# An attention and feed-forward block on one core: the last denominators by stream shuffles, the score bounds as 128 x 128, and a new tile table

## The chip, the cores and the metric

The kernel runs on one core of one Trainium2 chip. The time is the device time of the core in microseconds, the median of several runs. The profile comes from one execution, whose own time is given beside its span.

## The reference

```python
xn = layernorm(x)                       # x: 1 x 2048 x 512, bf16
q = (xn @ wq) -> 32 heads of 16;  k = xn @ wk;  v = xn @ wv   # one k and v of width 16 for all heads
p = softmax(q k^T / 4)                  # 32 x 2048 x 2048
A = (p v, heads joined) @ wo
B = gelu(xn @ w1 + b1) @ w2 + b2        # hidden width 1792
out = x + A + B
```

## The kernel before, in words

**Tiles.** Scores are made transposed: a tile has 128 keys on its rows and 512 columns of queries of one head. There are 2048 such tiles, in 32 groups of 64 tiles; a group has four heads (`j`, one in each 32-row block of PE's array) and sixteen key blocks. A unit `u` is three tiles that follow each other, three banks of PSUM; two sets of three banks alternate, so the scores (`scores`, L986) of a unit wait until the tiles two units earlier have been read.

**Two ways to the exponential.** The string `DTAB` says for each unit which of its tiles go to VectorE (DVE) rather than ScalarE (ACT). ACT takes its tiles of a unit in one instruction (`exp`, L1009). For a DVE tile, `p1` (L1040) turns the score into an integer whose bits are a rough exponential in bf16, and frees the bank. Up to six such tiles form a batch (`close_batch`), and additions (L1087 on DVE, two for a batch; L1083 one for each tile, on GpSimd (POOL) or DVE) make three shifted copies; five products with scaled values stand for one tile. A character of `DTAB` out of `CLOSE` ends a batch early. The products with V (`pv_mm`, L1053) add up in one bank, `pO`: each head has sixteen rows of output and one row, 16 of its 32, with the denominator.

**Score bounds.** Row 16 of each head's block in `QT` holds a bound that is subtracted from the scores. `q_pack` projects the queries of eight heads into bank 7 (`pM`), copies them out (`qp`, L1190), squares them (`sqq`, L1191) and spreads `qp` to `QT` by DMAs. `q_m` sums the squares with a selector `sel8R`, one matmul of 512 columns into 32 rows for each `p`, in the first of four column groups; DVE turns the sums into bounds (`mT`, L1203, 32 x 512), and four DMAs on SyncE's (SP's) queue put the rows into `QT`. `q_m` is called nine times, with 16 matmuls in all.

**Denominators.** For all groups but the last, `pO` is copied out (`o_evac` L1134, `o_quarter` L1100), the denominators go through DRAM to be inverted and spread, and a product follows (L1162, L1122; on POOL, or DVE where the planner puts it). The last group has `o_norm_last`: DVE copies `pO` in two halves (L1169), PE spreads the denominator row with a selector `selB` (f32, L675), ACT takes the logarithm (L1176) and the exponential of its negative (L1179), and DVE multiplies (L1182). Then sixteen matmuls with `wol`, a copy on ACT (L1407) and the last store follow.

**Order.** All work is recorded as operations with dependencies. `Prog.schedule` plays them through with assumed durations and picks by due time; the order found is the order of each engine's instructions, and `emit` adds the semaphores. The feed-forward work is spread over the units by the tables `HP` and `YP` (unit numbers). PE's idle gaps can be given filler matmuls (L1414). A planner constant, `C_OCC`, is what a 512-column matmul of one column group is taken to last.

Of the kernel before, what the change touches and what calls it, by code (L numbers as in the profile page):

```python
# [10 lines left out]
P = 128  # L11
# [13 lines left out]
C_OCC = 0.197  # L25
C_FIRST = 0.0105
WIN = 3.413
HAM_T = 0.35
# [34 lines left out]
CLOSE = "otABX"  # L63
DTAB = "tot00t2.0to2.o.0t20.o22ot02..t22t000ot..2o.o202.ot.02.o02oo2o.0oo0.00t.222t.2t2.o202.222t2o..2t0.ttt220o2.t.22.0o0o0.o2t.t02o0o.2t0t000.tt00.o2o0.2t0t.02oo22o.02o.22o2.o0o0..222o2ttttxxxB2t20.o20o0.o2t22oo2.t20o.ott0002.t0.t20.ot20oo02.t0200022t220.oo22.oo.t..o202t.t2o20to00..t022o0o0.20.t002.t0.0.022t.o2.0t.2t0t22t0.o0t.220o02t22.00o..2.22ot2.t0.2t0ot0t.02.oo0t22o20.0tt2220t.t02..0t222o.o0o.2t0o0ttt..20oo022t2.o0ot2..0oto.0t2t220o0t02.2oo20.2.o.22oo2o.o02.0o2t2t0.t.222o.o.2t2220ot..202o.02o0t0t2t.222tt022abXXAo02t22o0.o0..0o0o22t.t200tt2..t2t00ot.2o20ooo2o2.o20.o202.o.0t2to00ot2.t00ot0o.0.t.0tt020.t.oto2o02t2220.22o20t.2o0o202o.22..t22t00to202.0ooo2..0.0to.t2tt0o0ot0.t..0.."
YF = 664
# [12 lines left out]
QK = ((48,88.7,157.4),(45,107.7,130.4),(62,118.7,159.4))  # L78
HP = ((37,14,56.70835,151,34.34256,79.56046,20.54375,16.61271,55,117.24185,34.04239,145.57386,53.56559,74.35212),(146.29246,86.86647,89.5731,104.42399,169,0,0,0,0,0,0,0,0,0),(265,317.59193,277.51784,331,247,313,283,279.40403,337.07508,415,309.45685,269.66744,457,498.66805),(477.33471,482.59711,471.81669,494.32464,434.68696,0,0,0,0,0,0,0,0,0))
YP = ((199,183,217.4734,241),(346.51102,360.57108,380.86188,410.65667),(539.99266,523.90597,567.16436,582.95092),(593.39845,625,654.09462,657.83105))  # L80
GU = tuple((u, tbs, n, (("s", tbs[0], 0, 7), ("p", tbs[1], 5, 3), ("s", tbs[0], 7, 7), ("p", tbs[1], 8, 1), ("p", tbs[1], 9, 1),
# [24 lines left out]
TBW = 512  # L106
# [11 lines left out]
class Prog:  # L118
# [114 lines left out]
    def schedule(self):  # L233
# [43 lines left out]
        while left:  # L277
# [113 lines left out]
            if e == "pe":  # L391
                vleft -= op.kind == "v"
                s_seen = s_seen or vleft == 0
                st = t
                if op.kind in ("pv", "side"):
                    cg = op.tag[1]
                    st = max(t, cgbusy[cg], free["pe"])
                    if mode != "col":
                        st = r1 = max([t, pend + SW_COL] + [c + SW_COL for c in cgbusy])
                    op.start = st  # L400
                    cgbusy[cg] = st + (C_OCC + (C_FIRST if st < r1 + 0.1 else 0.0)) * slow
                    area += 0.0533
                    recent.append((st, 0.0533))
                    op.end = st + 0.006
                    op.vis = st + op.occ * slow + op.lat
                    mode = "col"
                    g = op.tag[0]
                if op.kind == "pv":
                    n = accn[g] = accn[g] - 1
                    s = started.setdefault(g, {})  # L410
                    s[cg] = s.get(cg, 0) + 1
                    op.tag = (g, cg, s[cg] == 1)
                    if len(s) == 4:
                        opened = g
                    if n == 0:
                        opened = None
                elif op.kind != "side":
                    m = {"S": "row", "side": "col"}.get(op.kind, "full")
                    w = 0.0 if m == mode else SW_ROW if m == "row" else SW_COL if m == "col" else SWITCH
                    st = max([t, pend + w] + [c + w for c in cgbusy])  # L420
                    op.start = st
                    op.end = st + op.occ * slow
                    op.vis = op.end + op.lat
                    area += op.occ * (0.75 if op.kind == "S" else 1.0)
                    recent.append((st, op.occ * (0.75 if op.kind == "S" else 1.0)))
                    if m == "col":
                        cgbusy = [op.end] * 4
                    mode = m
            else:
                op.start = t  # L430
                op.end = t + op.occ
                op.vis = op.end + op.lat
            if e == "pe":
                while op.start > wend:
# [3 lines left out]
                    area, wend = 0.0, wend + WIN  # L438
                pend = op.start + (C_OCC if op.kind in ("pv", "side") else op.occ) * slow
            if e == "act" and op.kind in ("exp", "gelu"):  # L440
# [30 lines left out]
    def settle(self):  # L471
        free = {e: 0.0 for e, _ in self.SECTIONS}
        mode, cg, pend, aend, r1 = None, [0.0] * 4, 0.0, 0.0, 0.0
        for op in self.ops:
# [3 lines left out]
            if op.eng == "pe":  # L478
                if op.kind in ("pv", "side") or (op.kind == "fill" and occ > 0.15):
                    if mode != "col":  # L480
                        t = r1 = max([t, pend + SW_COL] + [c + SW_COL for c in cg])
                    else:
                        t = max(t, cg[op.tag[1]])
                    cg[op.tag[1]] = t + C_OCC + (C_FIRST if t < r1 + 0.1 else 0.0)
                    mode, end = "col", t + 0.006
                else:
# [3 lines left out]
                    mode, end = m, t + occ  # L490
                pend = t + (C_OCC if mode == "col" else occ)
            else:
# [53 lines left out]
def bass_parallel_sum__grouped_kv_mqa__dense_activation_gelu__prompt_kernel(  # L546
# [33 lines left out]
    with ExitStack() as es:  # L580
# [28 lines left out]
        ident_f = sb([P, P], f32, "ident_f")  # L609
        selB = sb([P, P], f32, "selB")  # L610
        isc = sb([P, 1], f32, "isc")
# [38 lines left out]
        def bank(b, n=1):  # L650
            return pAll[:, b * 512:(b + n) * 512]
# [49 lines left out]
        def setup(fn, r=(), w=(), occ=0.16, due=0.0, lat=0.1, **kw):  # L701
# [23 lines left out]
        setup(lambda e: e.tensor_copy(ident_f[:], ident[:]), r=["ident"], w=["ident_f"], due=9.0)  # L725
        sel_diag = [bass.AP(sel8[:].tensor, sel8[:].offset + gl, [list(sel8[:].ap[0]), [34, NGR // 2], [8, HG]])
                    for gl in range(2)]
# [14 lines left out]
        for gl in range(2):  # L742
            setup(lambda e, gl=gl: e.tensor_copy(sel_diag[gl], mask8[:, 4 * gl:4 * gl + 4].unsqueeze(1).to_broadcast([P, NGR // 2, HG])),
                  r=["mask8", "sel8"], w=["sel8"], due=12.0)
# [178 lines left out]
        for v in KV_ORD:  # L923
# [5 lines left out]
            else:  # L929
# [4 lines left out]
        late = [pr.writer["ibi"]]  # L934
        setup(lambda e: e.tensor_copy(selB[:].rearrange("p (j r) -> p j r", j=4), ident[:, 16:113:32].unsqueeze(2).to_broadcast([P, 4, 32])),
              r=["ident"], w=["selB"], occ=0.3, due=24.0, after=late)
        dma("sp", wop[:], A_wo.rearrange("(g p) n -> p g n", p=P), "d_wo", w=["wop"], after=late)
# [228 lines left out]
        def o_norm_last(gg):  # L1166
            for h in range(2):
                c = slice(h * 256, h * 256 + 256)
                dve(lambda e, c=c: e.tensor_copy(Of[:, 1, c], pO[:, c]), w=["O", ("Of", 1), ("Of", 2 + h)], n=256, due=0.0)  # L1169
            for h in range(2):  # L1170
                c = slice(h * 256, h * 256 + 256)
                mm(bank(h)[:, 0:256], selB[:], Of[:, 1, c], True, True, r=[("Of", 2 + h), "selB"], w=[B(h)], occ=0.44, due=0.0)
            RB = [("rbP", 0, h, j) for h in range(2) for j in range(HG)]
            for h in range(2):
                c = slice(h * 256, h * 256 + 256)
                act(lambda e, h=h, c=c: e.activation(rbP[:, 0, c], bank(h)[:, 0:256], ACT.Ln), w=[B(h), ("rbl", h)] + RB, n=256, due=0.0)  # L1176
            for h in range(2):
                c = slice(h * 256, h * 256 + 256)
                act(lambda e, c=c: e.activation(rbP[:, 0, c], rbP[:, 0, c], ACT.Exp, scale=-1.0), w=[("rbl", h)], n=256, due=0.0)  # L1179
            for h in range(2):  # L1180
                c = slice(h * 256, h * 256 + 256)
                dve(lambda e, c=c: e.tensor_tensor(oT[:, c], Of[:, 1, c], rbP[:, 0, c], ALU.mult),  # L1182
                    r=[("Of", 2 + h), ("rbl", h)], w=[("oTl", h)], n=256, due=0.0)

# [14 lines left out]
        def q_m(ps, hqs):  # L1199
            for n, p in enumerate(ps):  # L1200
                mm(pM[0:32, :], sel8R[:, p, :], sqq[:, p % 2, :], n == 0, n == len(ps) - 1, r=["sel8R", ("sq", p % 2)],
                   w=[M4[0]], tp=(0, 0), kind="side", tag=(None, 0))
            dve(lambda e: e.tensor_scalar(mT[:].bitcast(i16), pM[0:32, :].bitcast(i32),  # L1203
                                          0.5 / 65536.0, float(0x1fc00000) / 65536.0, ALU.mult, ALU.add),
                w=M4 + ["mT"], allow=EV_ALLOW)
            h0, n = hqs[0], len(hqs)
            for j in range(HG):
                dma("sp", QT[32 * j + 16:32 * j + 17, h0:h0 + n, :], mT[8 * j + h0:8 * j + h0 + n, :], "d_m",
                    r=["mT"], w=[("QTm", hq, j) for hq in hqs])

# [242 lines left out]
```

## Time and profile before

| what | value |
|---|---|
| median of 3 runs | 744.11 us (744.03 to 744.12) |
| profiled execution | 743.81 us |
| its span | 742.1 us, 22084 instructions |
| PE busy | 729.0 us, 9117 matmuls |
| DVE busy | 727.0 us, 1374 instructions |
| ACT busy | 728.4 us, 759 instructions |
| POOL busy | 407.1 us, 554 instructions |
| granted TensorE clock | 1.000 |

Busy time counts what one or more instructions of an engine cover. Instructions overlap the ones behind them a little, so an engine can be held up by less than the overlap without showing idle time. In a row of groups stand the source line, engine, operation, output and inputs, shape and count, then busy microseconds and the mean nanoseconds of one, then the idle time ahead of them. In a row of the timeline stand start and length in microseconds.

### The profile page before, as it was taken

How to read it: one execution, taken by the hardware profiler on the slowest of the kernel's cores; microseconds unless marked ns; L12 is line 12 of the kernel's file. 1: busy time of each engine (PE TensorE's matmuls, PEld its weight loads, DVE VectorE, ACT ScalarE, POOL GpSimd, SP SyncE). 2: the span in 40 equal slices, each digit the busy share in tenths (PEclk: the TensorE clock that was granted, in tenths of full speed). 3: DMA queues.
4: the chain of work that ended last, by engine and by line, in shares of the span. 5: the costliest groups of instructions: out<-in, count | busy, mean ns of one | idle time of the engine just before them, and what ended most of it. 6: DMA issues, size and time to landing. Idle time of an engine off the chain costs nothing.

```text
span 742.1 us, 22084 instructions
## 1 busy us (share of the span) xinstructions
PE 729.0 (98%) x9117; PEld 229.8 (31%) x9117; DVE 727.0 (98%) x1374; ACT 728.4 (98%) x759; POOL 407.1 (55%) x554
## 2 busy tenths in 40 slices
PE   7999999999999999999999999999999999999998
PEld 4333322322243323222232323232233323223232
DVE  8899999999999999999999999999999999999995
ACT  8999999999999999999999999999999999999996
POOL 5565565666526565465566346564643575564642
PEclk9999999999999999999999999999999999999999
DMA  9200100100011020101101010010101101100010
GB/s 313 63 16 16 31 11 17 25 9 19 9 30 32 9 53 17 31 11 34 35 7 34 24 39 23 11 31 9 25 10 28 28 23 39 31 24 25 15 38 24
DMA packets 35963, 23.54 MB, mean 32 GB/s; under 512 B 17361, under 2 KB 32281, under 8 KB 35865
## 3 DMA queue, kind: packets, MB, share of 16 engines
q1 hardware_dynamic: 34808, 22.12, 11.6%
q8 instruction: 72, 1.18, 0.7%
q14 instruction: 27, 0.21, 0.1%
q10 hardware_dynamic: 1056, 0.03, 0.1%
HBM read 13.28 MB, written 2.35 MB: 21 GB/s over the span
## 4 chain that ended last, share of the span: by engine, by line
ACT 58%; PE 36%; DVE 5%; DMA 0%; issue 0%; SPq 0%
ACT E L1009 58%; PE pAll L1053 17%; PE pAll L986 11%; PE pAll L681 7%; DVE Dt L1040 1%; DVE Dt L1087 1%; DVE stats L770 1%; PE pAll L675 1%; DMA x_sb<-in_A_x_dram 0%; PE pAll L1414 0%; DVE ub L806 0%; ACT xnT L826 0%; DVE Dt L1083 0%; ACT ub L803 0%; DVE mv L784 0%
## 5 line engine op out<-in xcount | busy, mean ns | idle before, releaser
L1009 ACT ACTIVATE E<-pAll 128x1024 bf16<-128x1024 f32 (+1 forms) x678 | 675.6, 1187 | 2.7 <-PE pAll L986 2.5
L1083 POOL TENSOR_SCALAR Dt<-Dt 128x512 int16<-128x512 int16 x470 | 367.2, 781 | 301.5 <-DVE Dt L1087 130.3
L1053 PE MATMUL pAll<-Dt,V 128*32 128x512 bf16 x2845 | 430.5, 383 | 1.0 <-DVE Of L1134 0.8
L1040 DVE TENSOR_SCALAR Dt<-pAll 128x512 int16<-128x512 f32 x555 | 376.5, 694 | 2.3 <-PE pAll L986 1.1
L1087 DVE TENSOR_SCALAR Dt<-Dt 128x1024 int16<-128x1024 int16 (+8 forms) x514 | 292.4, 592 | 0.2
L1053 PE MATMUL pAll<-E,V 128*32 128x512 bf16 x1479 | 282.9, 385 | 0.0
L986 PE MATMUL pAll<-QT,KT 32*128 32x512 bf16 x2048 | 267.1, 384 | 2.8 <-ACT E L1009 1.6
L1053 PEld LDWEIGHTS pAll<-Dt,V 128*32 128x32 bf16 x2845 | 115.1, 94 | 120.9 <-issue 78.4
L986 PEld LDWEIGHTS pAll<-QT,KT 32*128 32x128 bf16 x2048 | 66.4, 90 | 275.6 <-ACT E L1009 257.7
L681 PE MATMUL pAll<-xnT,w_sb 128*32 128x512 bf16 x896 | 117.8, 382 | 0.0
L1053 PEld LDWEIGHTS pAll<-E,V 128*32 128x32 bf16 x1479 | 66.2, 94 | 44.0 <-issue 31.0
L681 PE MATMUL pAll<-w_sb,x_sb 128*32 128x512 bf16 x448 | 73.6, 381 | 0.0
L681 PE MATMUL pAll<-w_sb,ub 128*32 128x512 bf16 x448 | 72.6, 382 | 0.0
L681 PEld LDWEIGHTS pAll<-xnT,w_sb 128*32 128x32 bf16 x896 | 33.5, 95 | 21.8 <-issue 9.8
L681 PE MATMUL pAll<-wop,oTp 128*32 128x512 bf16 x192 | 34.7, 384 | 0.0
L1083 DVE TENSOR_SCALAR Dt<-Dt 128x512 int16<-128x512 int16 x99 | 25.5, 282 | 0.0
L1162 POOL TENSOR_TENSOR oTp<-OfP,rbP 128x256 bf16<-128x256 f32 x23 | 18.5, 814 | 7.6 <-DVE Dt L1087 4.4
L681 PE MATMUL pAll<-xnT,wq_sb 128*32 128x512 bf16 x256 | 21.1, 383 | 0.5 <-DVE ub L1218 0.5
L681 PEld LDWEIGHTS pAll<-w_sb,x_sb 128*32 128x32 bf16 x448 | 19.8, 95 | 4.0 <-issue 1.4
L1218 DVE TENSOR_SCALAR ub<-pAll,b1T 128x512 bf16<-128x512 f32 x28 | 20.8, 741 | 0.1
L681 PEld LDWEIGHTS pAll<-w_sb,ub 128*32 128x32 bf16 x448 | 19.2, 95 | 4.1 <-issue 2.3
L681 PE MATMUL pAll<-b2row,ones 128*32 128x512 bf16 x60 | 17.6, 383 | 0.0
(125 smaller groups left out, 273.9 us busy)
## 6 DMA issues: line engine op xcount, KB each, us to landing
w_sb<-in_B_w_dram SPq DMA_DIRECT2D x2, 1792.0 KB, 13.1
OfP<-Of SPq DMA_DIRECT2D x96, 32.0 KB, 1.9
rbP<-rden_rows SPq DMA_DIRECT2D x96, 32.0 KB, 1.8
x_sb<-in_A_x_dram SPq DMA_DIRECT2D x8, 256.0 KB, 4.3
x_sb<-in_A_x_dram SPq DMA_DIRECT2D x16, 128.0 KB, 2.3
QT<-qp SPq DMA_DIRECT2D x124, 16.0 KB, 1.8
out_dram<-x_sb SPq DMA_DIRECT2D x15, 128.0 KB, 1.9
OfP<-Of SPq DMA_DIRECT2D x56, 16.0 KB, 1.8
```

Source lines behind the costliest of these rows:

```text
L675: return add("pe", lambda e: e.matmul(o, l, rh, start=start, stop=stop, **kw), r, w, occ=occ, lat=dlat[1], allow=allow, **ak)
L681: add("pe", lambda e, c=c, j=j: e.matmul(o[c, :], l[:, c], rh, start=start, stop=stop, tile_position=(0, 32 * j)), r, [(k, j) for k in w] ...
L770: dve(lambda e, ti=ti, c=c: e.bn_stats(stats[:, c, :], x_sb[:, ti, :]), r=[("x", ti)], w=[("st", ti)], n=511, due=land(ti) + DU["sd"])
L986: ins = e.matmul(o, l, rh, start=True, stop=True, tile_position=(q0, 0))
L1009: o = act(lambda e: e.activation(E[:, s0:s0 + na, :], bank(b0, na).rearrange("p (a n) -> p a n", a=na), ACT.Exp, scale=LN2 / 128.0), w=[B( ...
L1040: op = dve(lambda e: e.tensor_scalar(Dt[:, s:s + n, :], bank(bk, n).rearrange("p (a n) -> p a n", a=n), float(127 * 128) + SPL_D, SPL_MIN, ...
L1053: add("pe", lambda e, a, b: e.matmul(pO[32 * j:32 * j + 32, :], V1[:, v, kt, :], rhs, start=a, stop=b, tile_position=(0, 32 * j)), r=r + [ ...
L1083: add("pool", lambda e, d=d, k=k: e.tensor_scalar(d, d, 1.0, float(k), ALU.mult, ALU.add), [], [(("D", base[o > 0] + q), o)], occ=PL_OCC, ...
L1087: dve(lambda e, d=view(o, nb), q=view(i, nb), k=k: e.tensor_scalar(d, q, float(k), None, ALU.add), r=keys(i), w=keys(o), n=nb * n * TBW, m ...
L1162: "pool", lambda e, c=c: e.tensor_tensor(oTp[0:n, sl, c], OfP[0:n, s, c], rbP[0:n, s, c], ALU.mult),
L1218: dve(lambda e: e.tensor_scalar(ubs[tb % 2][:, ft, :], pM, b1T[:, ft:ft + 1], None, ALU.add), r=["b1T"], w=M4 + [ukey(tb, ft)], n=TBW + 57 ...
```

## The change

Three things change.

1. `o_norm_last`: DVE no longer copies `pO`; two stream shuffles read it and write row 16 of every 32-row block to all 32 rows of `Of`. ACT's logarithm and exponential work on `Of` in place, and the products read `pO` itself. The matmuls with `selB`, and `selB`, go.
2. `q_m`: for each `p`, four matmuls of 128 columns, one in each column group, take the place of one of 512. The bounds stand as 128 rows x 128 columns (four query blocks by 32 groups and heads), one eviction of that shape; `sel_diag` orders the selector's columns to suit. Four DMAs, one for each query block, write four rows of `QT` at once; where only some groups are wanted, there are four for each.
3. The tables `DTAB`, `HP` and `YP` are replaced, and the planner is given 0.06 for a short matmul (`M_OCC`).

```diff
+M_OCC = 0.06
-DTAB = "tot00t2.0to2.o.0t20..."
+DTAB = "oto00t0t..2otttt.0o..."
...
-HP, YP = ...
+HP, YP = ...
...
-                    cgbusy[cg] = st + (C_OCC + (C_FIRST if st < r1 + 0.1 else 0.0)) * slow
+                    cgbusy[cg] = st + (min(op.occ, C_OCC) + (C_FIRST if st < r1 + 0.1 else 0.0)) * slow
...
-    sel_diag = [... [[34, NGR // 2], [8, HG]] ...]
+    sel_diag = [... [[80, 2], [34, 2], [4, HG]] ...]
-        mT = sb([32, TBW], bf, "mT")
+        mT = sb([P, P], bf, "mT")
...
         def o_norm_last(gg):
-            for h in range(2):
-                dve(tensor_copy(Of[:, 1, c], pO[:, c]))
-            for h in range(2):
-                mm(bank(h)[:, 0:256], selB[:], Of[:, 1, c])
-            for h in range(2):
-                act(activation(rbP[:, 0, c], bank(h)[:, 0:256], Ln))
-            for h in range(2):
-                act(activation(rbP[:, 0, c], rbP[:, 0, c], Exp, scale=-1.0))
-            for h in range(2):
-                dve(tensor_tensor(oT[:, c], Of[:, 1, c], rbP[:, 0, c], mult))
+            for h, c in enumerate(cs):
+                dve(stream_shuffle(Of[:, 1, c], pO[:, c], [16] * 32), n=300)
+            for h, c in enumerate(cs):
+                act(activation(Of[:, 1, c], Of[:, 1, c], Ln))
+            for h, c in enumerate(cs):
+                act(activation(Of[:, 1, c], Of[:, 1, c], Exp, scale=-1.0))
+            for h, c in enumerate(cs):
+                dve(tensor_tensor(oT[:, c], pO[:, c], Of[:, 1, c], mult))
...
         def q_m(ps, hqs):
             for n, p in enumerate(ps):
-                mm(pM[0:32, :], sel8R[:, p, :], sqq[:, p % 2, :], ..., tp=(0, 0))
-            dve(tensor_scalar(mT, pM[0:32, :], ...))
-            for j in range(HG):
-                dma("sp", QT[32 * j + 16:32 * j + 17, h0:h0 + n, :], mT[8 * j + h0:8 * j + h0 + n, :])
+                for c in range(4):
+                    mm(pM[32 * c:32 * c + 32, 0:P], sel8R[:, p, :], sqq[:, p % 2, P * c:P * c + P], ..., tp=(0, 32 * c), occ=M_OCC)
+            dve(tensor_scalar(mT, pM[:, 0:P], ...), n=P)
+            for c in range(4):
+                # n == 4: one DMA; otherwise one for each group of hqs
+                dma("sp", QT[16:113:32, h0:h0 + n, P * c:P * c + P], mT[32 * c + 4 * h0:32 * c + 4 * h0 + 16, :])
```

More of the change, by code (lines that the diff above doesn't have):

```diff
@@ L438, in schedule @@
                     area, wend = 0.0, wend + WIN
-                pend = op.start + (C_OCC if op.kind in ("pv", "side") else op.occ) * slow
+                pend = op.start + (min(op.occ, C_OCC) if op.kind in ("pv", "side") else op.occ) * slow
             if e == "act" and op.kind in ("exp", "gelu"):
@@ L483, in settle @@
                         t = max(t, cg[op.tag[1]])
-                    cg[op.tag[1]] = t + C_OCC + (C_FIRST if t < r1 + 0.1 else 0.0)
+                    cg[op.tag[1]] = t + min(occ, C_OCC) + (C_FIRST if t < r1 + 0.1 else 0.0)
                     mode, end = "col", t + 0.006
@@ L490, in settle @@
                     mode, end = m, t + occ
-                pend = t + (C_OCC if mode == "col" else occ)
+                pend = t + (min(occ, C_OCC) if mode == "col" else occ)
             else:
@@ L609, in bass_parallel_sum__grouped_kv_mqa__dense_activation_gelu__prompt_kernel @@
         ident_f = sb([P, P], f32, "ident_f")
-        selB = sb([P, P], f32, "selB")
         isc = sb([P, 1], f32, "isc")
@@ L725, in bass_parallel_sum__grouped_kv_mqa__dense_activation_gelu__prompt_kernel @@
         setup(lambda e: e.tensor_copy(ident_f[:], ident[:]), r=["ident"], w=["ident_f"], due=9.0)
-        sel_diag = [bass.AP(sel8[:].tensor, sel8[:].offset + gl, [list(sel8[:].ap[0]), [34, NGR // 2], [8, HG]])
+        sel_diag = [bass.AP(sel8[:].tensor, sel8[:].offset + gl, [list(sel8[:].ap[0]), [80, 2], [34, 2], [4, HG]])
                     for gl in range(2)]
@@ L934, in bass_parallel_sum__grouped_kv_mqa__dense_activation_gelu__prompt_kernel @@
         late = [pr.writer["ibi"]]
-        setup(lambda e: e.tensor_copy(selB[:].rearrange("p (j r) -> p j r", j=4), ident[:, 16:113:32].unsqueeze(2).to_broadcast([P, 4, 32])),
-              r=["ident"], w=["selB"], occ=0.3, due=24.0, after=late)
         dma("sp", wop[:], A_wo.rearrange("(g p) n -> p g n", p=P), "d_wo", w=["wop"], after=late)
@@ L1166, in o_norm_last @@
         def o_norm_last(gg):
-            for h in range(2):
-                c = slice(h * 256, h * 256 + 256)
-                dve(lambda e, c=c: e.tensor_copy(Of[:, 1, c], pO[:, c]), w=["O", ("Of", 1), ("Of", 2 + h)], n=256, due=0.0)
-            for h in range(2):
-                c = slice(h * 256, h * 256 + 256)
-                mm(bank(h)[:, 0:256], selB[:], Of[:, 1, c], True, True, r=[("Of", 2 + h), "selB"], w=[B(h)], occ=0.44, due=0.0)
-            RB = [("rbP", 0, h, j) for h in range(2) for j in range(HG)]
-            for h in range(2):
-                c = slice(h * 256, h * 256 + 256)
-                act(lambda e, h=h, c=c: e.activation(rbP[:, 0, c], bank(h)[:, 0:256], ACT.Ln), w=[B(h), ("rbl", h)] + RB, n=256, due=0.0)
-            for h in range(2):
-                c = slice(h * 256, h * 256 + 256)
-                act(lambda e, c=c: e.activation(rbP[:, 0, c], rbP[:, 0, c], ACT.Exp, scale=-1.0), w=[("rbl", h)], n=256, due=0.0)
-            for h in range(2):
-                c = slice(h * 256, h * 256 + 256)
-                dve(lambda e, c=c: e.tensor_tensor(oT[:, c], Of[:, 1, c], rbP[:, 0, c], ALU.mult),
-                    r=[("Of", 2 + h), ("rbl", h)], w=[("oTl", h)], n=256, due=0.0)
+            cs = [slice(h * 256, h * 256 + 256) for h in range(2)]
+            for h, c in enumerate(cs):
+                dve(lambda e, c=c: e.stream_shuffle(Of[:, 1, c], pO[:, c], [16] * 32), w=["O", ("Of", 1), ("rbl", h)], n=300, due=0.0)
+            for h, c in enumerate(cs):
+                act(lambda e, c=c: e.activation(Of[:, 1, c], Of[:, 1, c], ACT.Ln), w=[("rbl", h)], n=256, due=0.0)
+            for h, c in enumerate(cs):
+                act(lambda e, c=c: e.activation(Of[:, 1, c], Of[:, 1, c], ACT.Exp, scale=-1.0), w=[("rbl", h)], n=256, due=0.0)
+            for h, c in enumerate(cs):
+                dve(lambda e, c=c: e.tensor_tensor(oT[:, c], pO[:, c], Of[:, 1, c], ALU.mult),
+                    r=[("rbl", h)], w=[("oTl", h), "O"], n=256, due=0.0)
         def q_pack(tb, p, gls=(0, 1)):
```

25 lines of the change are left out of this document (15 added, 10 removed).

## The prediction

> **What bounds the kernel now.** I read the page first (busy shares, then the chain that ended last), then the waits, the groups by shape, and the timeline of the last 8 us.
>
> ```profile
> PE 729.0 (98%) x9117; PEld 229.8 (31%) x9117; DVE 727.0 (98%) x1374; ACT 728.4 (98%) x759; POOL 407.1 (55%) x554
> ...
> ACT 58%; PE 36%; DVE 5%; DMA 0%; issue 0%; SPq 0%
> ACT E L1009 58%; PE pAll L1053 17%; PE pAll L986 11%; PE pAll L681 7%; DVE Dt L1040 1%; DVE Dt L1087 1%; DVE stats L770 1%; PE pAll L675 1%; DMA x_sb<-in_A_x_dram 0%; PE pAll L1414 0%; DVE ub L806 0%; ACT xnT L826 0%; DVE Dt L1083 0%; ACT u
> ```
>
> Three engines are busy 98% of the span: no single one is the bound, and taking work from one helps only as far as the others can follow. The chain runs 58% through the exponentials (L1009), 36% through PE and 5% through DVE. Which of them paces a unit shows in the waits:
>
> ```profile
> PEld pAll L986 <- ACT E L1009: 257.7, 632, 0.8
> ```
>
> 632 times PE stood ready with the next scores and waited for ACT to release their banks. ACT is the pace, PE and DVE follow with little room, and what counts is (a) how much ACT has to do, (b) how often scores come late to it, (c) what is left after its last exponential.
>
> **(a) The number of tiles on ACT.** The table string marks 569 of the 2048 tiles for DVE before and 570 after. The number of ACT instructions stays at 678, so one tile is all that goes.
>
> ```profile
> L1009 ACT ACTIVATE E<-pAll 128x1024 bf16<-128x1024 f32 x547 | 524.9, 1110 | 2.2 <-PE pAll L986 2.0
> L1009 ACT ACTIVATE E<-pAll 128x1536 bf16<-128x1536 f32 x127 | 192.0, 1536 | 0.5 <-PE pAll L986 0.5
> ```
>
> A third tile in an instruction costs 1536 - 1110 = 426 ns: **-0.43 us** on ACT.
>
> **(b) What DVE gives and takes.** DVE must free score banks too, so its sum says whether ACT can keep its pace.
>
> ```profile
> L1040 DVE TENSOR_SCALAR Dt<-pAll 128x512 int16<-128x512 f32 x546 | 363.1, 681 | 2.3 <-PE pAll L986 1.1
> ...
> L1087 DVE TENSOR_SCALAR Dt<-Dt 128x1024 int16<-128x1024 int16 x170 | 69.3, 416 | 0.1
> ...
> L1087 DVE TENSOR_SCALAR Dt<-Dt 128x4096 int16<-128x4096 int16 x27 | 32.9, 1219 | 0.0
> ...
> L1083 DVE TENSOR_SCALAR Dt<-Dt 128x512 int16<-128x512 int16 x99 | 25.5, 282 | 0.0
> L1087 DVE TENSOR_SCALAR Dt<-Dt 128x512 int16<-128x512 int16 x85 | 23.8, 283 | 0.1
> ...
> L1203 DVE TENSOR_SCALAR mT<-pAll 32x512 int16<-32x512 int32 x9 | 6.0, 670 | 0.0
> ...
> L919 DVE COPY oTp<-pAll 128x224 f32<-128x224 f32 x1 | 0.4, 390 | 0.5 <-ACT oTp L851 0.5
> ```
>
> Durations overlap the next instruction; the spacing shows in one window of DVE's timeline, ahead of the longest wait of an exponential:
>
> ```profile
> 515.97 0.67 DVE L1203 TENSOR_SCALAR mT<-pAll 32x512 int16<-32x512 int32 x1
> 516.56 0.27 DVE L1087 TENSOR_SCALAR Dt<-Dt 128x512 int16<-128x512 int16 x1
> 516.76 0.67 DVE L1134 COPY Of<-pAll 128x512 f32<-128x512 f32 x1
> 517.36 0.67 DVE L1040 TENSOR_SCALAR Dt<-pAll 128x512 int16<-128x512 f32 x1
> ```
>
> From 516.76 to 517.36 is 0.60 for a duration of 0.67: each holds DVE for its duration less 0.07 to 0.08.
> - Removed: nine evictions of score bounds become 128x128. The nearest rows from PSUM are 390 ns at 224 columns and 681 at 512, about 1.0 ns a column, so 128 columns come to 0.29. That gives 9 x (0.67 - 0.29) = -3.4. If the time didn't fall with the columns it would be 0, at best 9 x 0.60 = -5.4; I take -3.4, as all PSUM rows shrink with their columns.
> - Added: the new table cuts 271 batches in place of 257 (the order of the built program has 28 more L1087 instructions). From 416 ns at 1024 and 1219 at 4096 columns, a column costs 0.26 ns and an instruction 0.15, of which 0.07 stays after the overlap: 28 x 0.07 + 1536 columns x 0.26 ns (the extra tile's three additions) = +2.4. Eight more L1083 move from POOL to DVE: 8 x 0.20 = +1.6. One tile more of L1040: +0.6. One product L1162 goes to POOL: -0.33 (shape and price of L1122, below).
> - Sum on DVE: -3.4 + 2.4 + 1.6 + 0.6 - 0.33 = **+0.9 us**. What the bounds save is spent on smaller batches; DVE's share of the chain is 5%, so +0.05 of it on the path.
>
> Where scores come late shows in three waits of ACT above 0.4 us during the exponentials:
>
> ```profile
> 99.17 1.02 ACT L1009 ACTIVATE E<-pAll 128x1024 bf16<-128x1024 f32 x1 [0.49 <-PE pAll L986]
> ...
> 518.74 1.02 ACT L1009 ACTIVATE E<-pAll 128x1024 bf16<-128x1024 f32 x1 [0.67 <-PE pAll L986]
> ...
> 678.39 1.45 ACT L1009 ACTIVATE E<-pAll 128x1536 bf16<-128x1536 f32 x1 [0.49 <-PE pAll L986]
> ```
>
> They sum to 1.65 us. The one at 518.74 ends a queue on DVE that the window above shows: bounds, an addition, the output copy, then the eviction that returns the bank. With the bounds 0.38 shorter those scores come 0.38 earlier. The new order keeps none of these places, so the bounds of this term are -1.65 (all three gone) and +0.9 (DVE's sum in full on the path). I take **-0.33**: that one eviction (-0.38), and DVE's share of its sum (+0.05).
>
> **The bounds on PE.** 16 matmuls of 512 columns in one column group become 64 of 128 columns in four, the same columns per group. At worst each of the 16 rounds holds PE like a full round of four long ones, 0.22 (the rounds at 737.22 and 737.44 below), in place of a quarter: 16 x 0.16 = +2.6. At best the unfilled groups of today are gone, -2.6. The planner's order lets other column groups work beside them, so I take 0. The extra DVE tile adds five products and removes one: four matmuls, one round, +0.2, where PE waits for ACT anyway. The bounds' DMAs go from 36 to 40 issues on SP, with four destinations each; SP has no share in the chain, and by the unit numbers in the code the bounds are made a group or more ahead of the scores that read them. If that cover were gone, scores would wait for a landing. The selector copy that leaves POOL had no waiter.
>
> **(c) The tail,** rows of DVE, ACT and PE in turn:
>
> ```profile
> 735.01 0.88 DVE L1169 COPY Of<-pAll 128x256 f32<-128x256 f32 x2 [2.35 <-PE pAll L1053]
> 735.81 0.41 DVE L1122 TENSOR_TENSOR xnT<-OfP,rbP 128x256 bf16<-128x256 f32 x1
> 737.65 0.76 DVE L1182 TENSOR_TENSOR oT<-Of,rbP 128x256 bf16<-128x256 f32 x2 [1.43 <-ACT rbP L1179]
> ```
> ```profile
> 736.44 0.88 ACT L1176 ACTIVATE rbP<-pAll 128x256 f32<-128x256 f32 x2 [1.98 <-PE pAll L675]
> 737.22 0.71 ACT L1179 ACTIVATE rbP<-rbP 128x256 f32<-128x256 f32 x2
> 739.31 0.60 ACT L1407 ACTIVATE ub<-pAll 128x512 bf16<-128x512 f32 x1 [1.38 <-PE pAll L681]
> ```
> ```profile
> 735.71 1.13 PE L675 MATMUL pAll<-Of,selB 128*128 128x256 f32 x4
> ...
> 737.22 0.59 PE L681 MATMUL pAll<-x_sb,ident 128*32 128x512 bf16 x2
> 737.44 0.81 PE L681 MATMUL pAll<-wop,xnT 128*32 128x512 bf16 x4
> 738.13 1.05 PE L681 MATMUL pAll<-xnT,oT 128*32 128x512 bf16 x16
> ```
>
> Today: copy at 735.01, four selector matmuls from 735.71, logarithm at 736.44, products from 737.65 to 738.41, last matmuls, copy at 739.31. After: the shuffle stands where the copy stood. No row shows a shuffle; the nearest is the copy of the same shape, and 0.88 for two gives 0.44. I take 0.43 and a hop of 0.03 (exponential to product today: 737.22 + 0.40 to 737.65). The first logarithm then starts at 735.47, 0.97 earlier. ACT now alternates logarithm and exponential by halves: 0.38 + 0.03 + 0.30 until the second logarithm can start, 0.38 + 0.03 + 0.41 to the second exponential's end, 737.00; product 737.03 to 737.45, against 738.41. PE must be ready by then: 29 matmuls (7.3 rounds, 1.6) from 734.7 end at 736.3, eight more on the product of L1122 at 736.7. So **-0.95**. With a shuffle of twice the copy's time it is -0.5; faster than the copy by half, -1.15.
>
> The Trainium skill (Vector Engine (DVE) Microarchitecture Reference, section 3.8) says a shuffle's lane selection is written by a load-mask instruction before it. No run here shows its price. DVE stands idle for 2.35 ahead of the first copy, so by that rule the first half loses nothing.
>
> **The sum.** Profiled execution 743.81 (span 742.1 and 1.7 around it): -0.43 - 0.33 - 0.95 = -1.71, so 742.1. The median of the runs lies 0.30 above the profiled one: **742.4 us**, 0.23% less.
>
> **Rivals.**
> - *DVE becomes the bound* (same). For: 98% busy, 0.9 more work. Then only the tail is gained, 744.11 - 0.95 + 0.9 = 744.1. Against: 5% of the chain, and long additions of 4096 columns and more, which block an eviction for over 1.2 us, fall from 39 to 33 in the new order. Chance 0.17.
> - *The waits of (b) vanish* (faster): 742.4 + 0.33 - 1.65 = 741.1. For: smaller batches. Against: new places make new waits. Chance 0.15.
> - *Slower: pile-ups at group ends.* The output copy, two evictions and an addition meet on DVE at the end of each of 31 groups; today three of them cost ACT 0.55 each. 271 batches and 35 more DVE instructions meet there more often. Four more such waits cancel the gain; six more give 742.4 + 3.3 = 745.7, over the bound. Against: the shorter bounds eviction. Chance 0.09.
> - *Short matmuls run one after another.* Then 64 take the spacing of the sixteen in the row at 738.13, (1.05 - 0.38)/15 = 0.045 each, 2.9 in place of 16 x 0.055 = 0.9: +2.0, 744.4. Against: that row itself, 16 in four groups within a microsecond. Chance 0.05.
>
> The Trainium skill (TensorE: Matmul & The Clock Gate, section Back-to-back issue gap) gives about 81 ns for each weight load and matmul of 128 columns; by it, an estimate, the 64 cost 5.2 and the time would be 746.7. The trace disagrees for column groups: 45 ns at four times the columns.
>
> That the change doesn't do what it says (a 128x128 eviction as dear as a 32x512 one) speaks against the row of 224 columns, and lies in the first rival.
>
> **Chances.** Forecast 0.54, rivals 0.17, 0.15, 0.09, 0.05. 0.2% is 1.5 us, about what a measurement of this kernel can tell from no change: the bounds are 742.6 and 745.6, and the forecast lies close to the first. Of its 0.54 I put 0.36 below 742.6 and 0.18 above. Faster 0.36 + 0.15 = 0.51; same 0.18 + 0.17 + 0.04 = 0.39; slower 0.09 + 0.01 = 0.10. Range: from the second rival (741.1) to the tail at its weak end with DVE's sum on the path (744.11 - 0.5 + 0.9 = 744.5), 741.0 to 744.5, which leaves out the slower cases and some at either end, under 2 in 10.
>
> **What would show it.** Right: L1203 near 0.29 and nine times; shuffles near 0.42; first logarithm about 0.5 after the first shuffle starts; 3.35 from the first shuffle's start to the start of ACT's last copy, in place of 4.30 (735.01 to 739.31); ACT waits above 0.4 no more than three. Wrong: L1203 still near 0.6, short matmuls spaced like long ones, more such waits of ACT, or DVE taking a tenth of the chain.

## The result, and the profile after

The changed kernel takes **742.2 us** (median of 11 runs, 741.92 to 742.69) against 744.09 (11 runs, 743.81 to 745.06): a ratio of 0.9974 with a 95% interval of 0.9964 to 0.9983, so 0.26% faster. The forecast was 742.4, its range 741.0 to 744.5. The profiled execution took 742.0, its span 740.3.

The page of the changed kernel, busy shares (busy us, share of the span, instructions) and the chain that ended last:

```profile
span 740.3 us, 22182 instructions
...
PE 724.7 (98%) x9145; PEld 228.2 (31%) x9145; DVE 726.8 (98%) x1411; ACT 728.0 (98%) x759; POOL 393.7 (53%) x547
...
ACT 63%; PE 32%; DVE 4%; DMA 0%; issue 0%; SPq 0%
```

The three engines are as full as before, in a span that is 1.8 us shorter (742.1 to 740.3). ACT has 5 points more of the chain, PE 4 less, DVE 1 less. The waits (total us, times, longest) say the same: PE stands for exponentials 642 times where it was 632.

```profile
PEld pAll L984 <- ACT E L1007: 261.4, 642, 0.9
```

The groups by shape (busy us, mean ns of one, idle before) answer to the terms of the sum:

```profile
L1007 ACT ACTIVATE E<-pAll 128x1024 bf16<-128x1024 f32 x544 | 522.0, 1116 | 1.6 <-PE pAll L984 1.5
...
L1007 ACT ACTIVATE E<-pAll 128x1536 bf16<-128x1536 f32 x128 | 193.5, 1535 | 0.6 <-PE pAll L984 0.6
...
L1085 DVE TENSOR_SCALAR Dt<-Dt 128x1024 int16<-128x1024 int16 x191 | 77.6, 418 | 0.1
...
L1085 DVE TENSOR_SCALAR Dt<-Dt 128x4096 int16<-128x4096 int16 x23 | 28.0, 1216 | 0.0
L1081 DVE TENSOR_SCALAR Dt<-Dt 128x512 int16<-128x512 int16 x107 | 27.5, 284 | 0.0
L1085 DVE TENSOR_SCALAR Dt<-Dt 128x512 int16<-128x512 int16 x99 | 27.5, 282 | 0.1
...
L1195 DVE TENSOR_SCALAR mT<-pAll 128x128 int16<-128x128 int32 x9 | 2.5, 277 | 0.0
```

The bounds' eviction (L1195) fell from 670 to 277 ns, and the additions (L1085 and L1081) took most of that time back: DVE's busy time is 726.8 in place of 727.0.

The tail, rows of DVE and then of ACT (start, us, instruction, idle before it and what ended it):

```profile
734.04 0.01 DVE L1167 LOAD_MASK_SELECT Of<-pAll  x1 [2.12 <-PE pAll L1051]
734.04 0.45 DVE L1167 STREAM_SHUFFLE Of<-pAll 128x256 f32<-128x256 f32 x1
734.53 0.01 DVE L1167 LOAD_MASK_SELECT Of<-pAll  x1
734.53 0.45 DVE L1167 STREAM_SHUFFLE Of<-pAll 128x256 f32<-128x256 f32 x1
734.88 0.41 DVE L1120 TENSOR_TENSOR xnT<-OfP,rbP 128x256 bf16<-128x256 f32 x1
735.42 0.42 DVE L1173 TENSOR_TENSOR oT<-pAll,Of 128x256 bf16<-128x256 f32 x1
736.30 0.42 DVE L1173 TENSOR_TENSOR oT<-pAll,Of 128x256 bf16<-128x256 f32 x1 [0.46 <-ACT Of L1171]
```
```profile
734.53 0.42 ACT L1169 ACTIVATE Of<-Of 128x256 f32<-128x256 f32 x1 [1.04 <-DVE Of L1167]
734.97 0.42 ACT L1171 ACTIVATE Of<-Of 128x256 f32<-128x256 f32 x1
735.30 0.40 ACT L1169 ACTIVATE Of<-Of 128x256 f32<-128x256 f32 x1
735.73 0.42 ACT L1171 ACTIVATE Of<-Of 128x256 f32<-128x256 f32 x1
737.53 0.60 ACT L1404 ACTIVATE ub<-pAll 128x512 bf16<-128x512 f32 x1 [1.38 <-PE pAll L681]
```

The logarithm follows the shuffle directly; the selector matmuls are gone. From the first shuffle to ACT's last copy are 737.53 - 734.04 = 3.49 us, where the copy of before needed 4.30.

To see which stage gained, I read from ACT's timelines the start of the first exponential of scores, the end of the last, and the start of ACT's last copy:

| profiled execution | first exponential | last one ends | stretch | last copy | tail |
|---|---|---|---|---|---|
| before | 24.10 | 734.47 | 710.37 | 739.31 | 4.84 |
| after | 24.09 | 733.49 | 709.40 | 737.53 | 4.04 |

So 0.97 us came out of the stretch of exponentials and 0.80 out of the tail; together 1.77 of the 1.8 by which the spans differ.

### The profile page after: what moved, and what is told of

It reads as the page before. It is cut to its first block, busy times and chain, and to the rows that moved or that the text cites. A ratio compares the mean times of both kernels' runs of the same rounds, so it can differ in the third digit from the quotient of the medians.

```text
span 740.3 us, 22182 instructions
## 1 busy us (share of the span) xinstructions
PE 724.7 (98%) x9145; PEld 228.2 (31%) x9145; DVE 726.8 (98%) x1411; ACT 728.0 (98%) x759; POOL 393.7 (53%) x547
## 4 chain that ended last, share of the span: by engine, by line
ACT 63%; PE 32%; DVE 4%; DMA 0%; issue 0%; SPq 0%
ACT E L1007 62%; PE pAll L1051 15%; PE pAll L984 9%; PE pAll L681 7%; DVE stats L770 1%; DVE Dt L1038 1%; DVE Dt L1085 1%; DMA x_sb<-in_A_x_dram 0%; PE pAll L675 0%; DVE Dt L1081 0%; DVE ub L806 0%; ACT xnT L826 0%; ACT ub L803 0%; DVE Of L1132 0%; PE pAll L1411 0%
## 5 line engine op out<-in xcount | busy, mean ns | idle before, releaser
L1081 POOL TENSOR_SCALAR Dt<-Dt 128x512 int16<-128x512 int16 x463 | 354.1, 765 | 311.2 <-DVE Dt L1085 137.3
L1051 PE MATMUL pAll<-Dt,V 128*32 128x512 bf16 x2850 | 422.4, 383 | 1.1 <-DVE Of L1132 1.1
L1038 DVE TENSOR_SCALAR Dt<-pAll 128x512 int16<-128x512 f32 (+1 forms) x555 | 377.3, 696 | 1.9 <-PE pAll L984 1.1
L1085 DVE TENSOR_SCALAR Dt<-Dt 128x1024 int16<-128x1024 int16 (+7 forms) x542 | 294.4, 571 | 0.1
L1051 PE MATMUL pAll<-E,V 128*32 128x512 bf16 x1478 | 276.0, 385 | 0.8 <-DVE Of L1132 0.8
L984 PEld LDWEIGHTS pAll<-QT,KT 32*128 32x128 bf16 x2048 | 66.5, 90 | 275.0 <-ACT E L1007 261.4
L1051 PEld LDWEIGHTS pAll<-Dt,V 128*32 128x32 bf16 x2850 | 112.4, 95 | 117.0 <-issue 70.9
L681 PE MATMUL pAll<-w_sb,ub 128*32 128x512 bf16 x448 | 70.3, 382 | 0.0
L681 PE MATMUL pAll<-w_sb,x_sb 128*32 128x512 bf16 x448 | 68.4, 382 | 0.0
L681 PE MATMUL pAll<-wop,oTp 128*32 128x512 bf16 x192 | 31.4, 384 | 0.0
L1081 DVE TENSOR_SCALAR Dt<-Dt 128x512 int16<-128x512 int16 x107 | 27.5, 284 | 0.0
L1132 DVE COPY Of<-pAll 128x512 f32<-128x512 f32 x24 | 16.3, 681 | 0.0
```

Of the source, the lines that this page charges most:

```text
L681: add("pe", lambda e, c=c, j=j: e.matmul(o[c, :], l[:, c], rh, start=start, stop=stop, tile_position=(0, 32 * j)), r, [(k, j) for k in w] ...
L984: ins = e.matmul(o, l, rh, start=True, stop=True, tile_position=(q0, 0))
L1038: op = dve(lambda e: e.tensor_scalar(Dt[:, s:s + n, :], bank(bk, n).rearrange("p (a n) -> p a n", a=n), float(127 * 128) + SPL_D, SPL_MIN, ...
L1051: add("pe", lambda e, a, b: e.matmul(pO[32 * j:32 * j + 32, :], V1[:, v, kt, :], rhs, start=a, stop=b, tile_position=(0, 32 * j)), r=r + [ ...
L1081: add("pool", lambda e, d=d, k=k: e.tensor_scalar(d, d, 1.0, float(k), ALU.mult, ALU.add), [], [(("D", base[o > 0] + q), o)], occ=PL_OCC, ...
L1085: dve(lambda e, d=view(o, nb), q=view(i, nb), k=k: e.tensor_scalar(d, q, float(k), None, ALU.add), r=keys(i), w=keys(o), n=nb * n * TBW, m ...
```

## Experiments

My theory was: the tail gains its full size by itself; in the stretch one tile less on ACT gains its own length, and DVE's time counts little, by its 5% of the chain. The main rival: DVE is as much the bound as ACT. Times are medians, with the kernel before at 743.86 to 743.98 beside them on the same chip. Beside the changed kernel's 742.2 it took 744.09, so a difference from 742.2 can be off by 0.1 to 0.2.

### The tail alone

The kernel before with the new `o_norm_last`, and nothing else:

```diff
-            dve(tensor_copy(Of[:, 1, c], pO[:, c])) ... mm(bank(h), selB, Of) ... act(Ln) ... act(Exp) ... dve(Of * rbP)
+            dve(stream_shuffle(Of[:, 1, c], pO[:, c], [16] * 32)) ... act(Ln) ... act(Exp) ... dve(pO * Of)
```

> The kernel before with the new tail alone (shuffles, no selector matmuls), old bounds, old tables; PE, DVE and ACT keep their order up to the last group. Theory (the tail is on the path on its own): the stretch up to the last exponential stays, the tail shortens by the 0.8 that the changed kernel shows, so 743.3. Rival (the gain is the table's, the tail is covered by PE's last matmuls): 744.1.

742.97 us (742.70 to 743.29), ratio 0.9988 (0.9979 to 0.9997): 0.9 gained. In the profiled execution the stretch stays (710.38, before 710.37) and the tail falls from 4.84 to 3.91. The theory holds: the tail is worth its size, and half of the whole gain is there.

### The bounds alone, the tables alone, and both new parts on the old tables

```diff
 # bounds alone: before, with the new q_m, mT, sel_diag and M_OCC; DTAB, HP, YP as before
 # tables alone: before, with the new DTAB, HP, YP
 # no new tables: after, with the old DTAB, HP, YP
```

> The kernel before with the new bounds alone (four column groups, 128x128 eviction), old tail, old tables. The planner replays the old tables with shorter bounds, so the order changes. Theory (what counts is where scores come late, and the old tables fit only the old durations): between 743.5 and 746, no gain of itself. Rival (DVE is the bound, and 9 x 0.39 = 3.5 less on it comes off the time): 740.6 to 742.

> The kernel before with the new tables alone, old bounds, old tail. DVE gets the smaller batches (+4.4) without what pays for them. Theory: slower than before by part of that, 744.5 to 747. Rival (the search alone brings the 1.0 of the stretch up to the last exponential): 743.1.

> The changed kernel with the old tables. Theory: the sum of the two parts alone, tail -0.8 and what the bounds alone give, so 0.8 less than that run; slower than the changed kernel by 1 to 4. Rival (the tables do nothing): 742.2.

Bounds alone 763.51 us (ratio 1.0259, 1.0241 to 1.0276), tables alone 784.72 (1.0548, 1.0534 to 1.0563), both new parts on the old tables 761.70 (1.0237, 1.0223 to 1.0251). Of the first two, both theory and rival missed by far. A row of the groups and one of the waits show most of the reason, first of the bounds alone, then of the tables alone:

```profile
L1084 DVE TENSOR_SCALAR Dt<-Dt 128x512 int16<-128x512 int16 x170 | 44.3, 285 | 0.0
```
```profile
ACT E L1010 <- PE pAll L1054: 12.5, 7, 3.5
```
```profile
L1083 DVE TENSOR_SCALAR Dt<-Dt 128x512 int16<-128x512 int16 x191 | 49.6, 285 | 2.9 <-PE pAll L1053 2.9
```
```profile
ACT E L1009 <- PE pAll L1053: 25.5, 11, 5.0
```

The planner replays the table against the durations that it is given. With a pair that wasn't searched together it moves additions from POOL to DVE (170 and 191, where before has 99 and after 107), and exponentials wait up to 3.5 and 5.0 us for products that haven't yet read the tile they overwrite, where the waits of before and after show exponentials waiting for scores alone. So these three runs tell what a mismatched order costs, 18 to 41 us, not what a part is worth. The tail is worth 1.8 between the first and third (763.51 - 761.70), but their own runs spread by 3.1 to 3.6, so that adds nothing to the run above. To price a part the order of instructions has to be held still; all later kernels do so.

### More work on one engine, in the order of after

Each keeps the changed kernel's order on every engine and adds work in nine places.

Nine evictions of the bounds at their old width (598 ns from one start to the next in place of 198: +3.6 on DVE):

```diff
-            dve(tensor_scalar(mT, pM[:, 0:P], ...))
+            dve(tensor_scalar(mT, pM[:, 0:4 * P], ...))
```

> The changed kernel in its own order, but each of the nine evictions of score bounds reads and writes 512 columns in place of 128 (three quarters of them unused), as long as before: +0.39 each, +3.5 on DVE. Theory (DVE frees the banks that ACT waits for, but has its share of the path only where scores come late): +0.5 to +1.5. Rival (DVE is the bound): +3 or more. Rival (DVE has room, the saving is worth nothing): within 0.3.

744.78 us (744.52 to 745.25): +2.6 over 742.2, 72% of what was added. That is between theory and rival, nearer to the rival.

Nine additions of 320 columns on DVE, beside evictions elsewhere in the groups (400 ns each, and up to 0.83 in four places: +3.6 to 5.2):

```diff
+                if more: e.tensor_tensor(spare[:], spare[:], spare[:], ALU.add)
                 return e.tensor_scalar(Dt[:, s:s + n, :], bank(bk, n), ...)
```

> The changed kernel in its own order, with nine extra DVE additions of 320 columns on a tile of no use, each ahead of an eviction of scores, in units far from the bounds: about 0.40 each, +3.6 on DVE. Theory (DVE is as near to the path everywhere as at the bounds, where three quarters of the time showed): +2.2 to +3. Rival (only the places of the bounds are tight): under +1.5.

745.59 us (745.25 to 745.90): +3.4, 65 to 94%, and more than the +3 that I had expected at most. The work costs no less at these nine places than at the bounds: DVE is near the path there too.

Nine activations of 368 columns on ACT (400 ns each, +3.6):

```diff
+                    if u in MORE: e.activation(spare[:], spare[:], ACT.Copy)
                     return e.activation(E[:, s0:s0 + na, :], bank(b0, na), ACT.Exp, scale=LN2 / 128.0)
```

> The changed kernel in its own order, with nine extra activations of 368 columns on a tile of no use, each ahead of an exponential near one of the nine evictions: about +0.36 each, +3.2 on ACT. Theory (ACT paces the stretch up to the last exponential): nearly all of it, +2.5 to +3.3. Rival (DVE or PE is the bound, ACT has room): under +1.5.

745.48 us (745.34 to 745.99): +3.3, 91%. As expected.

The 64 short matmuls stream 512 columns each (+2.5 on PE by the estimate below; PE's busy time rose by 2.0):

```diff
-                    mm(pM[32 * c:32 * c + 32, 0:P], ..., sqq[:, p % 2, P * c:P * c + P], ...)
+                    mm(pM[32 * c:32 * c + 32, :], ..., sqq[:, p % 2, P * c:P * c + P] four times over, ...)
```

> The changed kernel in its own order, but each of the 64 short matmuls streams 512 columns (its 128 four times), so that its 16 rounds cost a full round: 16 x (0.22 - 0.06) = +2.5 on PE. Theory (PE stands ready for ACT most of the time): +0.3 to +1.2. Rival (PE is the bound there): +2 or more.

742.87 us (742.71 to 743.45): +0.7, a quarter. PE has some room between the exponentials, so costing the short matmuls of the bounds at nothing was near enough.

### Less work on one engine

If DVE and ACT were each on the path, taking the same amount off one of them should give a good part of it. In the order of before, the nine evictions of the bounds at 128 columns (-3.6 on DVE); the rest of `mT` is set to zero once, on POOL during the setup:

```diff
-            dve(tensor_scalar(mT, pM[0:32, :], ...))
+            dve(tensor_scalar(mT[:, 0:P], pM[0:32, 0:P], ...))
```

> The kernel before in its own order, but each of the nine evictions of score bounds takes 128 of its 512 columns (the bounds of three quarters of the queries stay zero): -0.39 each, -3.5 on DVE. Theory (a shorter eviction helps most of the time, whatever the table, as the long one hurt in the changed kernel): -1.5 to -2.6, so 741.3 to 742.4. Rival (the old order has no use for it, the table must be searched anew first): within 0.5 of before.

743.76 us (743.44 to 746.06), ratio 1.0 (0.9991 to 1.0009): nothing that the medians can tell. Two rows show where DVE's time went, the shorter evictions and those of scores:

```profile
L1203 DVE TENSOR_SCALAR mT<-pAll 32x128 int16<-32x128 int32 x9 | 2.4, 269 | 0.0
```
```profile
L1040 DVE TENSOR_SCALAR Dt<-pAll 128x512 int16<-128x512 f32 x546 | 365.3, 685 | 3.8 <-PE pAll L986 2.1
```

DVE now stands idle for 3.8 us ahead of its evictions of scores, where the same row of before has 2.3; the scores end 2.1 of it, in place of 1.1. In the order of after, nine of the 24 copies of L1132 at 128 columns (-3.6 on DVE):

```diff
-            dve(tensor_copy(Of[:, i, :], pO))
+            dve(tensor_copy(Of[:, i, 0:cw], pO[:, 0:cw]))    # cw = 128 in nine groups
```

> The changed kernel in its own order, but nine of the output copies of DVE take 128 of 512 columns (those groups' outputs are left out in part): -0.40 each, -3.6 on DVE. Theory (ACT and DVE share the path; what DVE gives, ACT does not follow in full): -0.5 to -1.8. Rival (DVE alone is the bound): -3 or more.

742.29 us (742.04 to 742.58): nothing again, though the groups show the copies shortened as meant, and again DVE waits longer ahead of its evictions (3.5; the changed kernel has 1.9):

```profile
L1134 DVE COPY Of<-pAll 128x128 f32<-128x128 f32 x9 | 2.5, 281 | 0.0
```
```profile
L1039 DVE TENSOR_SCALAR Dt<-pAll 128x512 int16<-128x512 f32 x544 | 363.7, 685 | 3.5 <-PE pAll L985 2.0
```

And nine exponentials over one tile in place of two (-3.8 on ACT):

```diff
-                o = act(activation(E[:, s0:s0 + na, :], bank(b0, na), Exp))
+                o = act(... if u not in LESS else activation(E[:, s0:s0 + 1, :], bank(b0), Exp))
```

> The changed kernel in its own order, but nine exponentials take one tile of their two (the other tile is left out): -0.43 each, -3.8 on ACT. Theory (ACT paces, but DVE is close behind it): -1 to -2.5. Rival (ACT alone is the bound): -3.5 or more; rival (DVE alone): under -0.5.

741.76 us (741.58 to 741.84): -0.4, a tenth. The waits of this kernel, PE's for exponentials and ACT's for scores:

```profile
PEld pAll L985 <- ACT E L1008: 255.4, 628, 0.9
```
```profile
ACT E L1008 <- PE pAll L985: 3.4, 10, 0.5
```

PE waits 6.0 less for ACT (261.4 in the changed kernel), and ACT waits 1.2 more for scores than in the changed kernel, whose own row is:

```profile
ACT E L1007 <- PE pAll L984: 2.2, 5, 0.5
```

The starts of the exponentials show where the 3.8 went. After one tile the next exponential can start 0.49 us later, after two tiles 0.90, by the shortest spacings in the traces. After the nine shortened ones it started 0.65 to 1.03 later, 7.66 us in all against 9 x 0.904 = 8.14: it could use 0.48 of the 3.8.

The medians hold the setup too, and the first exponential starts anywhere from 23.94 to 24.40 us in these profiles, of which each kernel has one. The stretch from the first exponential to the end of the last leaves the setup out. In two pairs of kernels that share the code of the stretch it agrees within 0.01 us: before and the tail alone (710.36 and 710.37), after and logarithms first below (709.39 and 709.40). These are sums of the trace's nanoseconds, and so can differ by 0.01 from the table above.

| profiled execution | work added (us) | first exponential | stretch | change of the stretch |
|---|---|---|---|---|
| after | | 24.09 | 709.39 | |
| wider evictions | DVE +3.6 | 24.27 | 712.09 | +2.69, 75% |
| additions on DVE | DVE +3.6 to 5.2 | 24.12 | 712.75 | +3.35, 64 to 93% |
| activations on ACT | ACT +3.6 | 23.94 | 712.88 | +3.49, 97% |
| long matmuls | PE +2.5 | 23.99 | 710.24 | +0.85, 34% |
| shorter copies | DVE -3.6 | 24.30 | 709.40 | +0.01, nothing |
| shorter exponentials | ACT -3.8 | 24.03 | 708.92 | -0.47, 12% |
| before | | 24.10 | 710.36 | |
| before, shorter evictions | DVE -3.6 | 24.40 | 710.05 | -0.32, 9% |

So three removals missed my expectation: one gained nothing, two about a tenth of what was taken off. Taken with the additions: in a fixed order a longer instruction on DVE or ACT costs 64 to 97% of itself, a shorter one gives a tenth or nothing. Scores go by turns to ACT and DVE through the same banks. An engine that is late holds the others; one that is early finds the next bank not yet filled, as its longer waits for scores show.

### Both logarithms first

The changed tail with ACT in the order logarithm, logarithm, exponential, exponential:

```diff
-            act(Ln, half 0); act(Exp, half 0); act(Ln, half 1); act(Exp, half 1)
+            act(Ln, half 0); act(Ln, half 1); act(Exp, half 0); act(Exp, half 1)
```

> The changed kernel with ACT's tail in the order logarithm, logarithm, exponential, exponential, all else the same. In the changed kernel the second exponential starts 1.20 after the first logarithm, since each exponential waits for the logarithm just ahead of it. With both logarithms first the second can start as its shuffle ends (0.49 after the first), the exponentials 0.28 and 0.31 behind it, so the second product starts at 1.54 in place of 1.78 after the first logarithm: -0.2, 742.0. Rival (PE's last products or the shuffle hold it): no change.

742.00 us (741.82 to 742.35) against 742.2, which these runs don't tell apart. DVE's timeline of this kernel:

```profile
735.87 0.88 DVE L1173 TENSOR_TENSOR oT<-pAll,Of 128x256 bf16<-128x256 f32 x2 [0.49 <-ACT Of L1171]
```

The products now stand back to back, the first 0.45 later than in the changed kernel (735.87 against 735.42), and end at 736.75 (736.72 there), although the shuffles began 0.10 later (734.14 in place of 734.04). It is the fastest version that keeps the whole computation, within the noise.

## Why the prediction was right

- **(a) One tile less on ACT, -0.43.** The shapes are as said: 128 exponentials of 1536 columns in place of 127, no more instructions in all. With the shortest spacing after each shape (904 ns after two tiles, 1330 after three, 494 after one) the new counts come to 0.39 less, which is one part of the 0.97 by which the stretch fell. No run takes this part alone, and in the held order 3.8 us less on ACT gave only 0.4 to 0.5.
- **(b) DVE and the waits, -0.33.** What remains of the stretch is 0.97 - 0.39 = 0.58. That is more than said, and the way to it was wrong in two steps; that the forecast held in spite of them is luck.
  The first step is "with the bounds 0.38 shorter those scores come 0.38 earlier". The profile of before puts the late start of those scores (518.29) down to ACT itself, whose exponential before ended at 515.59 + 2.48 = 518.07.

```profile
515.59 2.48 ACT L1009 ACTIVATE E<-pAll 128x1024 bf16<-128x1024 f32 x2
518.74 1.02 ACT L1009 ACTIVATE E<-pAll 128x1024 bf16<-128x1024 f32 x1 [0.67 <-PE pAll L986]
```
```profile
518.29 0.10 PEld L986 LDWEIGHTS pAll<-QT,KT 32*128 32x128 bf16 x3 [0.42 <-ACT E L1009]
```

  With the bounds shortened in that order, the eviction behind them moved by 0.17 only (517.36 to 517.19), since it now waited for its own scores, and the exponential waited 0.67 as before:

```profile
515.94 0.27 DVE L1203 TENSOR_SCALAR mT<-pAll 32x128 int16<-32x128 int32 x1
516.13 0.27 DVE L1087 TENSOR_SCALAR Dt<-Dt 128x512 int16<-128x512 int16 x1
516.33 0.67 DVE L1134 COPY Of<-pAll 128x512 f32<-128x512 f32 x1
517.19 0.69 DVE L1040 TENSOR_SCALAR Dt<-pAll 128x512 int16<-128x512 f32 x1 [0.18 <-PE pAll L986]
```
```profile
518.70 1.02 ACT L1009 ACTIVATE E<-pAll 128x1024 bf16<-128x1024 f32 x1 [0.67 <-PE pAll L986]
```

  The second step is "DVE's share of the chain is 5%, so +0.05 of it on the path": added work on DVE cost 64% of itself or more. The sum of +0.9 on DVE came out at -0.2 (busy 727.0 to 726.8), so the wrong price did no harm. Counting each instruction up to the start of the next, the bounds gave 3.6 (3.4 said), L1085 took 2.1 more (2.4 said), L1081 1.1 (1.6 said), L1038 0.2 (0.6 said), the product gave 0.33 as said, and small changes elsewhere add 0.3.
  Three waits of ACT above 0.4 us were to remain at most, and three there are, at new places; three rows of ACT's timeline and, ahead of the second of them, DVE's:

```profile
225.43 1.02 ACT L1007 ACTIVATE E<-pAll 128x1024 bf16<-128x1024 f32 x1 [0.48 <-PE pAll L984]
...
431.19 1.45 ACT L1007 ACTIVATE E<-pAll 128x1536 bf16<-128x1536 f32 x1 [0.49 <-PE pAll L984]
...
699.28 1.02 ACT L1007 ACTIVATE E<-pAll 128x1024 bf16<-128x1024 f32 x1 [0.49 <-PE pAll L984]
```
```profile
429.41 0.68 DVE L1038 TENSOR_SCALAR Dt<-pAll 128x512 int16<-128x512 f32 x1
430.01 0.68 DVE L1132 COPY Of<-pAll 128x512 f32<-128x512 f32 x1
430.61 0.68 DVE L1038 TENSOR_SCALAR Dt<-pAll 128x512 int16<-128x512 f32 x1
```

  At 431.19 and 699.28 a copy and evictions stand ahead on DVE, as in the pile-up that the prediction names; at 225.43 there is no copy, and ACT comes from a table load and a single tile. In all three, as in the three of before, the profile has the scores start 0.04 to 0.05 us after the end of ACT's exponential before (0.22 at 518.74). So it is not shown that the pile-up on DVE makes these waits.
  The gain of (b) lies in these long waits. Beyond the shortest spacing of each shape, the starts of exponentials lost 11.86 us before and 11.22 after, leaving out three gaps with other work of ACT. The gaps that lost over 0.4 were four before (0.92, 0.78, 0.71 and 0.45) and are three after (0.71, 0.64 and 0.59), 0.91 less in all; the others lost 0.27 more. That leaves 0.64, and the record of the last exponential is 0.07 longer.
- **The short matmuls, 0.** Right. PE's timeline around a set of them:

```profile
122.42 0.24 PE L675 MATMUL pAll<-sqq,sel8R 128*32 128x128 bf16 x3
122.48 0.38 PE L1051 MATMUL pAll<-Dt,V 128*32 128x512 bf16 x2
...
122.64 0.22 PE L675 MATMUL pAll<-sqq,sel8R 128*32 128x128 bf16 x1
```

  Three start within 0.02 us of each other (0.24 for durations of 0.22), the next product 0.06 behind the first of them, and the fourth 0.22 behind it. So the rival of matmuls one after another falls. The Trainium skill gives about 81 ns for each weight load and matmul of 128 columns (TensorE: Matmul & The Clock Gate, section Back-to-back issue gap). For matmuls in different column groups these rows disagree with it.
- **(c) The tail, -0.95.** Right in mechanism, 0.14 too large by the two traces: 0.81 (4.30 to 3.49), and 0.9 by the run of it alone. The shuffle took 0.45 (0.43 said), the first logarithm started 0.49 after it (0.46), the second product 1.77 after that (1.56): a logarithm from SBUF took 0.40 to 0.42 where I had 0.38, the time of one from PSUM, and the last product started 0.15 after its exponential ended, where I had 0.03. The load-mask instruction that the Trainium skill names (Vector Engine (DVE) Microarchitecture Reference, section 3.8) is there, 0.01 each in the rows, the first of them under DVE's idle 2.12.
- **The sum.** -0.43 - 0.33 - 0.95 against -0.97 - 0.80 in the traces: 1.71 said, 1.77 seen. The stretch gave 0.21 more than said and the tail 0.15 less, so the sum is nearer than its terms.
- **The rivals.** "DVE becomes the bound" did not come, since the new order left DVE's sum as it was; but its premise is right: with 3.6 more on DVE in the same order the time is 744.8 to 745.6. Long waits did not vanish, and no more pile-ups came. At the 72% of the widened evictions, the 0.9 which I feared on DVE would have cost 0.65, and left a gain of some 1.2 us. The forecast was right also because that term came out at nothing, which is luck.

What stays open is how the 0.58 of (b) divides between shorter evictions and the new table, and why the new order has fewer long waits. The two were searched together, and neither gives the gain without the other: old widths in the new order cost 2.6, new widths in the old order bring 0.3 of the stretch, and the new table with the old durations costs 40.9.

## What to carry to other kernels

Where three engines are 98% busy in lock-step, the chain's shares say who was last, not what a microsecond is worth: here added work cost 64 to 97% on either of the two engines that share the score banks, and removed work gave a tenth or nothing. So measure an edit in both directions, in a held order, and don't count on a shorter instruction until the order is searched anew with its duration. A table that was searched for other durations cost 18 to 41 us here, over ten times what any part is worth. A step in the tail, with nothing beside it, was worth its full size and could be read off the rows.

## What the runs showed of the hardware

- A shuffle of 128x256 f32 from PSUM took 0.45 us, about as long as a copy of that shape (0.42 in the profile of before), and its load-mask instruction 0.01.
- Three matmuls of 128 columns in different column groups started within 0.02 us of each other, and 64 such at four times the columns cost 0.7 us in all.
- A transfer of the bounds that writes four rows took less of SP's time to issue than one that writes one: by the tile view a median of 526 ns (40 issues), 588 before (36).

```profile
L688 SPq DMA_DIRECT2D QT<-mT x40: 497/526/592, 32.0 to 578.2; - x40
```

- The same addition of 320 columns on DVE took 0.48 to 0.49 us in five places and 0.81 to 0.90 in the other four. In these four an addition on POOL was under way when it started, ran on for 0.47 to 0.57, and DVE's ended 0.33 to 0.34 after it. In the five, POOL was idle at the start, or done within 0.10. One of the four, in the rows of DVE and of POOL:

```profile
303.35 0.90 DVE L1044 TENSOR_TENSOR spare<-spare 128x320 f32<-128x320 f32 x1
```
```profile
303.18 0.73 POOL L1089 TENSOR_SCALAR Dt<-Dt 128x512 int16<-128x512 int16 x1 [2.77 <-DVE Dt L1045]
```
